# Halving additions, a copy on ScalarE and more first-load tiles in the block inverse of a recurrent attention with a mixture of experts

## The chip, the cores and the metric

The kernel runs on one core of a Trainium2 chip. The core has TensorE (PE, matrix multiplications, with PEld for its weight loads), VectorE (DVE), ScalarE (ACT), GpSimd (POOL) and SyncE (SP, which mostly issues DMA transfers). Each engine works through its own list of instructions in order and waits at an instruction whose operands are not ready. The metric is device time in microseconds (us) of one execution. Where the text speaks of the clock, it is the share of TensorE's full clock that the profile shows as granted.

## The reference

The inputs r, k, v, w, a and b have the shape (4 batches, 8 heads, 768 steps, 40 channels), float32. For each batch and head a state of 40 x 40 runs through the steps:

```python
for t in range(S):
    y[:, :, t] = einsum('bhd,bhde->bhe', rt, state)
    Sa = einsum('bhde,bhe->bhd', state, at)
    state = state * wt[:, :, None, :] - einsum('bhd,bhe->bhde', Sa, bt) + einsum('bhd,bhe->bhde', vt, kt)
```

The 3072 x 320 result goes through eight experts of two layers (320 to 1024, relu, 1024 to 320). Their outputs are summed with weights P, which come from x @ w_gate by eight rounds of normalising over rows and columns in turn.

## The kernel before, in words

**Chunks.** The 768 steps are cut into 12 chunks of 64. A pair of chunk c and batch b, numbered cb = 4c + b, is the unit of work; its eight heads are four pairs. There are two kinds of work for each unit.

**Preparation** (`prep`, line 106) does not depend on the state. It loads one block of 450 KB (line 109), makes the running products of the decays with two scans on VectorE (q, line 113, and gf, line 123), scales k, b and a with them (kb, line 137; ab, lines 143 and 144), multiplies them into a 64 x 64 triangle on TensorE (ll, line 149), transposes kb (kt, line 157) and writes masked copies into the tile set of that unit (sx, line 159; lines 145, 146 and 164 to 166). The lower triangle lt goes to DRAM (ld, lines 152 and 168). There are 20 tile sets. The first units have no tile of their own for the load: `IN_SEQ` lets units 0 to 3 load into sets 19 to 16, which no unit uses yet, units 4 and 5 into the two ordinary `inp` tiles, and units 6 and 7 into sets 19 and 18 again.

**Inverse.** For two chunks at a time (a group, `GROUPS`) the 32 x 32 diagonal blocks of all triangles, 128 in number, lie one to a partition: `load_lu` reads them from DRAM (lu, line 351), and VectorE inverts them (un). `inv_diag` (lines 171 to 177) does the 8 x 8 blocks column by column; `inv_off` then joins them with eight calls of `contract` (line 179) for a group, each with one product of 512, 1024 or 2048 elements for each partition (line 183, pr; four of 512, two of 1024 and two of 2048) and one reduction over the inner index (line 186). `finish` makes a turned copy tn, which lies in the same tile as pr (line 340), and writes un and tn to DRAM (ud and nd, lines 342 and 343). `tload` reads them back in the layout of the matrix multiplications (td and tt, lines 215 to 221) and `tmat` joins two 32 x 32 blocks into one 64 x 64 inverse on TensorE (gp, line 230; op, line 235).

**Recurrence** (`recur`, line 239). For each unit, in five steps with a yield between them: av (line 259), masked on VectorE into f (line 260); xc (line 267) with the set's sx; pu (line 278) with the inverse tt, masked into pm (line 280); c (line 285) with the set's bb, added into ws on VectorE (line 287); y and z on GpSimd (lines 291 and 302; z on VectorE from chunk 9); and the transpose zt (line 307), which carries the state on. Four batches go side by side.

**What sets the order.** The list `ev` (line 355) gives each piece of work a time on a scale where one chunk of recurrence is 5; the functions are called in that order, and a scheduler then places the instructions in each engine's list. `P0` and `PD` set the preparations of a group against the recurrence, `INV_DT` spaces the steps of an inverse, and `T_CLEAR` places the zeroing of fixed tiles. After the attention the experts follow; from their eighth block on, the order is the one in which the code is written.

Of the kernel before, what the change touches and what calls it, by code (L numbers as in the profile page):

```python
# [11 lines left out]
F32 = mybir.dt.float32  # L12
F32R = mybir.dt.float32r
AF = mybir.ActivationFunctionType
ALU = mybir.AluOpType
AX = mybir.AxisListType
# [4 lines left out]
NP = 4  # L21
R2 = 104
RP = 112
# [6 lines left out]
def attention(ctx, tc, d, xd, ps, pq, pt, gs, lg):  # L30
    nc = tc.nc
    pin = ctx.enter_context(tc.tile_pool(name="a_in", bufs=1))
# [19 lines left out]
    for n in range(NCH * NB - NSX, NCH * NB):  # L52
        i, pool = n % NSX, sets[n - NCH * NB + NSX]
        if i in IN_SETS or i in KB_SETS:
            raw = pool.tile([128, 1252], F32, name=f"st{i}")
# [19 lines left out]
    un, lu, tn = (t[:, 0:1024].rearrange("u (a b) -> u a b", b=32) for t in (unf, luf, prf))  # L75
# [5 lines left out]
    def clear():  # L81
        nc.gpsimd.memset(unf, 0.0)
        nc.gpsimd.memset(unf[:, 0:1024:33], 1.0)
        for t in vz_b + c1_b + lg_b:
            nc.vector.memset(t, 0.0)
        for t in tt_b:
            nc.gpsimd.memset(t, 0.0)
    fresh = set(range(NSX))

    def first_use(i):  # L90
        if i in fresh:
            fresh.discard(i)
            nc.gpsimd.memset(bb_b[i], 0.0)
            nc.scalar.copy(out=sx_b[i][64:R2].rearrange("r p h x -> r (p h) x")[:, :, 64:104],
                           in_=cst[64:R2, 360:400].unsqueeze(1).broadcast_to([40, 8, 40]))
# [3 lines left out]
    def rot(key, lst):  # L99
        i = state[key]  # L100
        state[key] = (i + 1) % len(lst)
        return lst[i]
# [3 lines left out]
    def prep(c, b, ld):  # L106
        cb = c * NB + b
        inp = raws[IN_MAP[cb]][0:RP, 0:1029] if IN_MAP.get(cb) else pin.tile([RP, 1029], F32, name="inp", bufs=2)
        nc.sync.dma_start(out=inp, in_=d["inp"][c, b])
        kb_in = inp[0:R2, 261:773].rearrange("r (p k t) -> r p k t", p=NP, k=2)  # L110
        a_in = inp[0:R2, 773:1029].rearrange("r (p t) -> r p t", p=NP)
        qf = pin.tile([RP, NP, 65], F32, name="q")
        nc.vector.tensor_tensor_scan(  # L113
            out=qf.rearrange("r p t -> r (p t)"), data0=inp[:, 0:260], data1=one65,
            initial=0.0, op0=ALU.mult, op1=ALU.add)
        q = qf[0:R2]
        g1 = rot("g1", g1_b)
        nc.vector.reciprocal(out=g1[:, :, 64], in_=qf[:, :, 64])
        sx = rot("sx", sx_b)
        i = next(j for j in range(NSX) if sx_b[j] is sx)  # L120
        bb, cc = bb_b[i], cc_b[i]
        gf = pin.tile([RP, NP, 65], F32, name="gf", bufs=2)
        nc.vector.tensor_tensor_scan(  # L123
            out=gf.rearrange("r p t -> r (p t)")[:, 259::-1], data0=inp[:, 260:0:-1],
            data1=g1.rearrange("r p t -> r (p t)")[:, 259::-1], initial=0.0, op0=ALU.mult, op1=ALU.add)
        gd[c, b] = dr1.tile([RP, 260], F32, name=f"gd{cb}")
        nc.sync.dma_start(out=gd[c, b], in_=gf.rearrange("r p t -> r (p t)"))
        g = gf[0:R2, :, 64:0:-1]
        if cb < NKB:
            raw = raws[KB_SETS[cb % len(KB_SETS)]]  # L130
            kb = raw[0:R2, 0:512].rearrange("r (p k t) -> r p k t", p=NP, k=2)
            lt = raw[0:64, 512:1024].rearrange("r (p k t) -> r p k t", p=NP, k=2)
        else:
            kb = pin.tile([R2, NP, 2, 64], F32, name="kb")
            lt = pin.tile([64, NP, 2, 64], F32, name="lt")
        eng = nc.vector if cb < NFAST else nc.gpsimd
        (nc.gpsimd if cb in KB_POOL else eng).tensor_tensor(
            out=kb, in0=kb_in,
            in1=q[:, :, 63::-1].unsqueeze(2).broadcast_to([R2, NP, 2, 64]), op=ALU.mult)
        ab = rot("ab", ab_b)  # L140
        first_use(i)
        nc.gpsimd.tensor_copy(out=cc, in_=q[:, :, 64])
        eng.tensor_tensor(out=ab[0:40, :, 0:64], in0=a_in[0:40], in1=g[0:40], op=ALU.mult)
        eng.tensor_tensor(out=ab[64:104, :, 64:128], in0=a_in[64:104], in1=g[64:104], op=ALU.mult)  # L144
        nc.scalar.copy(out=sx[64:104, :, 0, 0:64], in_=ab[0:40, :, 0:64])
        nc.scalar.copy(out=sx[64:104, :, 1, 0:64], in_=ab[64:104, :, 64:128])
        ll = pq.tile([128, NP, 2, 64], F32, name="ll", tag="pq")
        for p in range(NP):
            nc.tensor.matmul(ll[:, p], lhsT=kb[:, p], rhs=ab[:, p], start=True, stop=True)  # L149
        if cb < NKB:  # L150
            nc.scalar.activation(out=lt, in_=ll[64:128], func=AF.Copy, scale=-1.0)
            (nc.sync if cb < N_SP else nc.scalar).dma_start(out=ld[GRP[c][1], :, b], in_=lt)
            kt = pt.tile([128, NP, 2, 64], F32, name="kt", tag="pt")
        else:
            kt = pq.tile([128, NP, 2, 64], F32, name="kt", tag="pq")
        for p in range(NP):
            nc.tensor.transpose(kt[:, p].rearrange("s h x -> s (h x)")[:, 0:R2],
                                kb[:, p].rearrange("r k s -> r (k s)"), ident[0:R2, 0:R2])
        nc.vector.tensor_tensor(
            out=sx[0:64, :, :, 0:64], in0=ll[0:64],  # L160
            in1=mask_u.unsqueeze(1).unsqueeze(1).broadcast_to([64, NP, 2, 64]), op=ALU.mult)
        if cb >= NKB:
            nc.scalar.activation(out=lt, in_=ll[64:128], func=AF.Copy, scale=-1.0)
        nc.scalar.copy(out=sx[0:64, :, :, 64:104], in_=kt[0:64, :, :, 0:40])
        nc.scalar.activation(out=bb[0:64, :, 0:40], in_=kt[64:128, :, 0, 0:40], func=AF.Copy, scale=-1.0)
        nc.scalar.activation(out=bb[64:128, :, 64:104], in_=kt[64:128, :, 1, 0:40], func=AF.Copy, scale=-1.0)
        if cb >= NKB:
            (nc.sync if cb < N_SP else nc.scalar).dma_start(out=ld[GRP[c][1], :, b], in_=lt)
        return dict(cc=cc, sx=sx, bb=bb)
# [9 lines left out]
    def contract(us, dst, a, m):  # L179
        nu = us.stop - us.start  # L180
        n_c, n_r, n_k = a.shape[1], m.shape[2], a.shape[2]
        prv = prf[us, 0:n_c * n_r * n_k].rearrange("u (c k r) -> u c k r", r=n_r, k=n_k)
        nc.vector.tensor_tensor(  # L183
            out=prv, in0=a.unsqueeze(3).broadcast_to([nu, n_c, n_k, n_r]),
            in1=m.unsqueeze(1).broadcast_to([nu, n_c, n_k, n_r]), op=ALU.mult)
        nc.vector.tensor_reduce(out=dst, in_=prv.rearrange("u c k r -> u c r k"), op=ALU.add, axis=AX.X)  # L186

    def inv_off(us, o, n, h):
        gt = gtf[us, 0:n * n].rearrange("u (c r) -> u c r", r=n)
# [147 lines left out]
                   dr.tile([128, 32, 32], F32, name="ud"), dr.tile([128, 32, 32], F32, name="nd")]  # L337

    def finish(s, us):
        nc.vector.tensor_copy(out=tn[us], in_=un[us].rearrange("u c s -> u s c"))  # L340
        for o in range(0, us.stop, 64):
            nc.sync.dma_start(out=invs[s][1][o:o + 64], in_=un[o:o + 64])
            nc.sync.dma_start(out=invs[s][2][o:o + 64], in_=tn[o:o + 64])

    def load_lu(s, n):
        ld = invs[s][0]
        for cc in range(n):
            for blk in range(2):
                for h in range(2):
# [2 lines left out]
                        out=lu[u0:u0 + 16],  # L352
                        in_=ld[cc, r0:r0 + 32].rearrange("j b p h s -> (b p) j h s")[:, :, h, r0:r0 + 32])

    ev = [(T_CLEAR, clear, ())]
    gens = {}
    def step(c, b):
        if (c, b) not in gens:
# [8 lines left out]
    for c in range(NCH):  # L367
        for b in range(NB):
            for k in range(5):
                ev.append((5 * c + k + SKEW * b, step, (c, b)))  # L370
        t = 5 * c + 2 - T_LEAD
        ev.append((t - L_LEAD, tload, (c,)))
        for half in range(2):
            ev.append((t + 2 * SKEW * half, tmat, (c, half)))
    for s, cs in enumerate(GROUPS):
        us = slice(0, 64 * len(cs))
        t0 = 5 * cs[0] - 10
        n = len(cs) * NB
        for i in range(n):
            cb = (cs[0] + i // NB, i % NB)  # L380
            j = cb[0] * NB + cb[1] - NSX
            t = 5 * (j // 4) + 3 + SKEW * (j % 4) + 0.01
            t = max(t, t0 + P0 + PD * i) if s else -20 + 0.01 * i
            ev.append((t, do_prep, (s,) + cb + (i == 0,)))
        t += 0.02
        ev.append((t, load_lu, (s, len(cs))))
        for i, (fn, a) in enumerate(INV):
            ev.append((t + INV_DT * i, fn, (us,) + a))
        ev.append((t + INV_DT * 10 + 0.01, finish, (s, us)))
    for _, fn, args in sorted(ev, key=lambda x: x[0]):  # L390
# [5 lines left out]

GROUPS = [[0, 1], [2, 3], [4, 5], [6, 7], [8, 9], [10, 11]]
GRP = {c: (i, j) for i, g in enumerate(GROUPS) for j, c in enumerate(g)}
P0 = -8
PD = 0.75  # L400
INV_DT = 0.05
SKEW = 1.1
NSX = 20
GL = 1
# [2 lines left out]
NFB = 3  # L407
NRB = 2
KB_POOL = (1,2,3,4,5,6,7)
IN_SETS = (19, 18, 17, 16)  # L410
KB_SETS = (15, 14, 13, 12)
IN_SEQ = (19,18,17,16,0,0,19,18)
IN_MAP = dict(enumerate(IN_SEQ))
N_SP = 8
NKB = 6
NFAST = 6
T_CLEAR = -19.95
PC = 4
PQ = 2
PT = 2  # L420
T_LEAD = 2
L_LEAD = 0.5
NWS = 4
NK = (2 * E - 1) * (NF // 2)
# [386 lines left out]
```

## Time and profile before

| | us |
|---|---|
| median of 3 runs | 1846.83 (1845.23 to 1849.42) |
| the profiled execution, its own time | 1847.82 |
| its span, first to last instruction | 1846.0 |
| mean granted TensorE clock | 0.954 |
| TensorE busy in the span | 1734.9 |
| VectorE busy in the span | 1397.2 |

The page shows the span in 40 slices of 46 us; a digit is a tenth of the slice. The attention takes about the first eleven slices, where VectorE is as busy as TensorE or busier and the clock digit is under 9 in most of them; the experts take the rest, where TensorE is busy throughout. The span and the profiled execution's own time differ by 1.8 us, which lie around the span.

### The profile page before, as it was taken

Reading aid. Unit: us, or ns where it says so; the run is one execution under the profiler, and the core shown is the slowest. Engines: PE = TensorE matmul, PEld = TensorE weight load, DVE = VectorE, ACT = ScalarE, POOL = GpSimd, SP = SyncE. Lnnn points to the kernel's source line nnn. Section 1 sums busy time; section 2 is a strip of 40 time slices with the busy share of each in tenths; the row PEclk is TensorE's granted clock in tenths of the full one; section 3 lists DMA queues with packets and bytes.
Section 4 is the critical chain, followed back from the end, with each engine's and each line's share of the span. In section 5 each row is a group of like instructions: output and inputs, shape, how many; then the busy total and the mean of one; then the engine's idle time right before and its main releaser. Section 6 shows DMA issues by size and latency. Waiting matters only on the chain.

```text
span 1846.0 us, 31552 instructions
## 1 busy us (share of the span) xinstructions
PE 1734.9 (94%) x11843; PEld 1705.9 (92%) x11843; DVE 1397.2 (76%) x2306; ACT 855.9 (46%) x1848; POOL 873.1 (47%) x848
## 2 busy tenths in 40 slices
PE   5479898999989999999999999999999999999999
PEld 4378788899888999999999999999999999999999
DVE  7877969768698768677786868977686877778675
ACT  6347666666643534344343443445343443435342
POOL 6535556441572618355371826006291744628170
PEclk8569988889899999999999999999999999999999
DMA  8467787875720102011110202201020111102001
GB/s 211 116 152 177 184 183 181 182 173 133 203 82 31 56 1 75 20 56 38 38 56 19 75 20 67 65 14 57 19 75 19 57 38 38 57 19 75 5 34 43
DMA packets 194957, 145.10 MB, mean 79 GB/s; under 512 B 143861, under 2 KB 171637, under 8 KB 194805
## 3 DMA queue, kind: packets, MB, share of 16 engines
q1 hardware_dynamic: 191125, 137.35, 28.3%
q10 hardware_dynamic: 3680, 5.74, 1.1%
q8 instruction: 94, 1.54, 0.4%
q14 instruction: 58, 0.48, 0.1%
HBM read 117.00 MB, written 26.04 MB: 77 GB/s over the span
## 4 chain that ended last, share of the span: by engine, by line
PE 76%; DVE 10%; DMA 6%; issue 4%; ACT 2%; POOL 2%; SPq 1%; DVEq 0%; ACTq 0%; POOLq 0%
PE op L620 36%; PE p L555 33%; DMA inp<-in_inp_dram 2%; PE xc L267 2%; DVE pr L183 2%; DVE gt L186 1%; PE pu L278 1%; DVE q L113 1%; PE c L285 1%; PE av L259 1%; DVE un L186 1%; DMA ld<-lt 1%; DVE gf L123 1%; DMA rb<-in_r_dram 1%; DVE hl L579 1%
## 5 line engine op out<-in xcount | busy, mean ns | idle before, releaser
L555 PE MATMUL p<-xch,wh 128*128 128x384 f32 (+1 forms) x1792 | 605.7, 339 | 9.2 <-DVE sm L573 5.6
L576 ACT ACTIVATE hh<-sm 128x384 fp32r<-128x384 f32 x512 | 269.4, 526 | 726.4 <-DVE sm L573 726.2
L620 PE MATMUL op<-wh,hh 128*128 128x320 f32 x1536 | 476.8, 311 | 1.0 <-ACT hh L576 0.9
L620 PE MATMUL op<-wl,hh 128*128 128x320 f32 x1536 | 474.6, 309 | 0.0
L620 PE MATMUL op<-wh,hl 128*128 128x320 f32 x1536 | 467.1, 309 | 0.7 <-DVE hl L579 0.7
L501 POOL TENSOR_TENSOR wl<-ws,wh 128x640 fp32r<-128x640 f32 x60 | 103.6, 1727 | 608.5 <-ACT wh L499 608.3
L579 DVE SCALAR_TENSOR_TENSOR hl<-sm,hh 128x384 fp32r<-128x384 f32 x512 | 375.6, 767 | 2.4 <-ACT hh L576 2.0
L555 PEld LDWEIGHTS p<-xch,wh 128*128 128x128 f32 (+1 forms) x1792 | 337.4, 188 | 13.4 <-DVE sm L573 6.8
L555 PE MATMUL p<-xcl,wh 128*128 128x384 f32 x896 | 302.5, 338 | 0.0
L555 PE MATMUL p<-xch,wl 128*128 128x384 f32 x896 | 301.8, 337 | 0.0
L620 PEld LDWEIGHTS op<-wh,hh 128*128 128x128 f32 x1536 | 290.2, 189 | 1.6 <-ACT hh L576 1.5
L620 PEld LDWEIGHTS op<-wl,hh 128*128 128x128 f32 x1536 | 291.0, 189 | 0.0
L620 PEld LDWEIGHTS op<-wh,hl 128*128 128x128 f32 x1536 | 286.9, 188 | 1.1 <-DVE hl L579 0.9
L573 DVE TENSOR_TENSOR sm<-p,u 128x384 f32<-128x384 f32 x384 | 234.3, 621 | 8.8
L555 PEld LDWEIGHTS p<-xcl,wh 128*128 128x128 f32 x896 | 168.7, 188 | 0.0
L555 PEld LDWEIGHTS p<-xch,wl 128*128 128x128 f32 x896 | 168.6, 188 | 0.0
L573 DVE TENSOR_TENSOR sm<-p,p 128x384 f32<-128x384 f32 x128 | 71.2, 557 | 128.5 <-PE p L555 76.5
L573 DVE TENSOR_TENSOR p<-p,p 128x384 f32<-128x384 f32 x128 | 71.1, 555 | 98.7 <-PE p L555 98.0
L573 DVE TENSOR_TENSOR u<-p,p 128x384 f32<-128x384 f32 x128 | 70.8, 553 | 59.7 <-PE p L555 58.6
L509 POOL TENSOR_TENSOR wl<-ss,wh 128x512 fp32r<-128x512 f32 x60 | 89.9, 1498 | 32.7 <-ACT wh L506 28.4
L149 PE MATMUL ll<-ab,kb 104*128 104x128 f32 x336 | 64.0, 350 | 43.8 <-POOL ab L144 22.2
L291 POOL TENSOR_TENSOR y<-ws,gr 104x256 f32<-104x256 f32 x48 | 49.5, 1031 | 117.3 <-DVE ws L287 95.0
(156 smaller groups left out, 2774.4 us busy)
## 6 DMA issues: line engine op xcount, KB each, us to landing
ws<-in_wts_dram SPq DMA_DIRECT2D x60, 832.0 KB
inp<-in_inp_dram SPq DMA_DIRECT2D x42, 450.2 KB
rb<-in_r_dram SPq DMA_DIRECT2D x48, 224.0 KB
gd<-gf SPq DMA_DIRECT2D x48, 113.8 KB
gr<-gd SPq DMA_DIRECT2D x48, 113.8 KB
vz<-in_v_dram SPq DMA_DIRECT2D x48, 112.0 KB
ld<-lt ACTq DMA_DIRECT2D x40, 128.0 KB
f<-in_vt_dram SPq DMA_DIRECT2D x48, 80.0 KB
```

The lines of the kernel that those rows point to most:

```text
L149: nc.tensor.matmul(ll[:, p], lhsT=kb[:, p], rhs=ab[:, p], start=True, stop=True)
L183: nc.vector.tensor_tensor(out=prv, in0=a.unsqueeze(3).broadcast_to([nu, n_c, n_k, n_r]), in1=m.unsqueeze(1).broadcast_to([nu, n_c, n_k, n_ ...
L186: nc.vector.tensor_reduce(out=dst, in_=prv.rearrange("u c k r -> u c r k"), op=ALU.add, axis=AX.X)
L267: nc.tensor.matmul(xc[h][:, p], lhsT=pp["sx"][:, p, h], rhs=f[:, p, h], start=True, stop=True)
L291: nc.gpsimd.tensor_tensor(out=y[:, :, b % 2], in0=ws[:, :, 0:64], in1=gr[0:R2, :, 64:0:-1], op=ALU.mult)
L501: g.tensor_tensor(out=wl[:, 0:640], in0=raw[:, 256:896], in1=wh[:, 0:640], op=ALU.subtract)
L509: g.tensor_tensor(out=lv[:, 3:7], in0=so[:, :, 0], in1=hv[:, 3:7, 0], op=ALU.subtract)
L555: nc.tensor.matmul(o, lhsT=w_, rhs=x_, start=(j == 0), stop=(j == 3))
L573: eng.tensor_tensor(out=out, in0=x, in1=y, op=ALU.add)
L576: nc.scalar.activation(out=hh[:, f, h], in_=sm[f][:, h], func=AF.Relu)
L579: v.scalar_tensor_tensor(out=hl[:, f, h], in0=sm[f][:, h], scalar=0.0, in1=hh[:, f, h], op0=ALU.max, op1=ALU.subtract)
L620: nc.tensor.matmul(ops[i], lhsT=a[:, h, cs], rhs=w_[:, cw], start=(f == 0 and h == 0 and j == 0), stop=(last and h == 1 and j == 2))
```

## The change

It has these parts:

- In `contract` the reduction is replaced by halving additions: the inner index of n_k (8 or 16) is cut in half and the halves added, in place in pr, until one is left, which goes to the destination. A call with n_k = 8 issues three additions, one with 16 issues four.
- The turned copy tn in `finish` is made on ScalarE and not on VectorE.
- The first eight units each have a tile set to load into (sets 19 to 12), the sets that hold their kb and lt are 11 to 8, and all eight are prepared in the manner that was used for the first six (`NKB`, `NFAST`). The tile q has two buffers (`NQF`).
- The zeroing of un and of the VectorE tiles is placed at -20.01, that of tt in a function of its own at -19.915.
- The numbers that place the work: `P0` from -8 to -10, `INV_DT` from 0.05 to 0.2, and `T_FIRST` = 0 in place of 5 * 0 + 2 - 2 for chunk 0, which is the same value.

```diff
@@ attention
+    def clear_tt():
         for t in tt_b:
             nc.gpsimd.memset(t, 0.0)
@@ prep
-        qf = pin.tile([RP, NP, 65], F32, name="q")
+        qf = pin.tile([RP, NP, 65], F32, name="q", bufs=NQF)
@@ contract
-        nc.vector.tensor_reduce(out=dst, in_=prv.rearrange("u c k r -> u c r k"), op=ALU.add, axis=AX.X)
+        while n_k > 1:
+            n_k //= 2
+            nc.vector.tensor_tensor(out=dst if n_k == 1 else prv[:, :, 0:n_k],
+                                    in0=prv[:, :, 0] if n_k == 1 else prv[:, :, 0:n_k],
+                                    in1=prv[:, :, 1] if n_k == 1 else prv[:, :, n_k:2 * n_k], op=ALU.add)
@@ finish
-        nc.vector.tensor_copy(out=tn[us], in_=un[us].rearrange("u c s -> u s c"))
+        nc.scalar.copy(out=tn[us], in_=un[us].rearrange("u c s -> u s c"))
@@ the list of events
-    ev = [(T_CLEAR, clear, ())]
+    ev = [(T_CLEAR, clear, ()), (T_CLEAR2, clear_tt, ())]
-        t = 5 * c + 2 - T_LEAD
+        t = 5 * c + 2 - T_LEAD if c else T_FIRST
@@ the numbers
-P0 = -8
+P0 = -10
-INV_DT = 0.05
+INV_DT = 0.2
-IN_SETS = (19, 18, 17, 16)
-KB_SETS = (15, 14, 13, 12)
-IN_SEQ = (19,18,17,16,0,0,19,18)
+IN_SETS = (19, 18, 17, 16, 15, 14, 13, 12)
+KB_SETS = (11, 10, 9, 8)
+IN_SEQ = (19, 18, 17, 16, 15, 14, 13, 12)
-NKB = 6
-NFAST = 6
-T_CLEAR = -19.95
+NKB = 8
+NFAST = 8
+T_CLEAR = -20.01
+T_CLEAR2 = -19.915
+NQF = 2
+T_FIRST = 0
```

The scheduler places everything anew. Three places of its lists matter below; line numbers of the changed kernel are two to nine higher than those of the kernel before.

SP's list at the start of the program, before: st and inp are the loads of the units (a number behind st names the tile set), vz, rb and f the first tiles of the recurrence.

```order
L109 DMA st_173<-in_inp_dram 112x1029
L109 DMA inp<-in_inp_dram 112x1029 x2
L242 DMA vz_208<-in_v_dram 112x4x64
L245 DMA rb<-in_r_dram 112x512
L250 DMA f<-in_vt_dram 64x8x40
L242 DMA vz_209<-in_v_dram 112x4x64
L245 DMA rb<-in_r_dram 112x512
```

The same place in the changed kernel:

```order
L111 DMA st_164<-in_inp_dram 112x1029
L111 DMA st_163<-in_inp_dram 112x1029
L111 DMA st_162<-in_inp_dram 112x1029
L111 DMA st_161<-in_inp_dram 112x1029
L111 DMA inp<-in_inp_dram 112x1029 x2
L248 DMA vz_200<-in_v_dram 112x4x64
L251 DMA rb<-in_r_dram 112x512
L256 DMA f<-in_vt_dram 64x8x40
```

Ten unit loads, and not six, now stand ahead of the first vz and rb.

VectorE's list at the end of the first inverse, before: the reduction into un of 128x16x8 is the last step of the inverse, and the two rows of 128x4 begin the next inverse.

```order
L186 TENSOR_REDUCE un<-pr 128x16x8
L123 SCALAR_TENSOR_TENSOR gf<-inp,g_207 112x260
L113 SCALAR_TENSOR_TENSOR q<-inp,cst 112x260
L340 COPY pr<-un 128x1024
L118 RECIPROCAL g_207<-q 112x4
L123 SCALAR_TENSOR_TENSOR gf<-inp,g_207 112x260
L159 TENSOR_TENSOR st_172<-ll,cst 64x8x64
L159 TENSOR_TENSOR st_173<-ll,cst 64x8x64
L174 TENSOR_TENSOR pr<-un,lu 128x4
L177 TENSOR_REDUCE un<-pr 128x4
```

The same place in the changed kernel, from the last product of the first inverse on:

```order
L185 TENSOR_TENSOR pr<-gt,un 128x2048
L115 SCALAR_TENSOR_TENSOR q<-inp,cst 112x260
L161 TENSOR_TENSOR st_165<-ll,cst 64x8x64
L115 SCALAR_TENSOR_TENSOR q<-inp,cst 112x260
L190 TENSOR_TENSOR pr<-pr 128x16x64
L120 RECIPROCAL g_199<-q 112x4
L190 TENSOR_TENSOR pr<-pr 128x16x32
L125 SCALAR_TENSOR_TENSOR gf<-inp,g_199 112x260
L190 TENSOR_TENSOR pr<-pr 128x16x16
L120 RECIPROCAL g_199<-q 112x4
L190 TENSOR_TENSOR un<-pr 128x16x8
L125 SCALAR_TENSOR_TENSOR gf<-inp,g_199 112x260
```

The copy is gone from this list, four additions stand where one reduction stood, and rows of preparations stand between them. From the first row of the first inverse to its last, the list before holds five q, five gf and six sx rows, the changed one eight q, seven gf and eight sx rows. After one gf and one sx row the second inverse begins in the changed list, and the first row pm of the recurrence comes 34 rows behind that beginning; before, the first pm stood 19 rows behind it. The later inverses end, counted in units of the recurrence ahead of the first that needs them, 3, 5, 4, 4 and 4 units early in the changed list, and 4, 3, 3, 3 and 2 before.

TensorE's list between the first inverse and the first pu, before:

```order
L149 MATMUL ll<-ab_206,kb 128x128 x4
L157 MATMUL kt<-cst,kb 128x104 x4
L230 MATMUL gp<-td,lg 64x32 x8
L149 MATMUL ll<-ab_205,kb 128x128 x4
L157 MATMUL kt<-cst,kb 128x104 x4
L235 MATMUL op<-td,lg 64x32 x8
L230 MATMUL gp<-td,lg 64x32 x8
L278 MATMUL pu<-x_924,tt_201 128x104 x4
```

The same place in the changed kernel:

```order
L151 MATMUL ll<-ab_197,kb 128x128 x4
L159 MATMUL kt<-cst,kb 128x104 x4
L236 MATMUL gp<-td,lg 64x32 x8
L241 MATMUL op<-td,lg 64x32 x8
L236 MATMUL gp<-td,lg 64x32 x8
L284 MATMUL pu<-x_1019,tt_193 128x104 x4
```

The preparation that stood between gp and op is gone from there. Ahead of the first pu the list now holds the ll of 19 units, and before of 17.

## The prediction

> **What bounds the kernel now.** I read the page's slices first, then busy time by stage, then who is waited for in the stages that are not full. The clock's row of the page's slices (40 of 46 us each, tenths), below 9 only in the first eleven:
>
> ```profile
> PEclk8569988889899999999999999999999999999999
> ```
>
> Busy time in four of the five stages that I cut at the first inverse (55), the first pu (111), the first expert products (505) and the end of the transition; the columns are busy us of PE, PEld, DVE, ACT and POOL, granted clock, DMA share and GB/s:
>
> ```profile
> 0.00:55.00 55.00, 28.59 (x152) 25.38 (x152) 36.67 (x67) 33.27 (x81) 34.97 (x61) 0.78 0.84 203
> 55.00:111.00 56.00, 23.91 (x130) 21.70 (x131) 44.71 (x64) 19.66 (x50) 28.32 (x27) 0.50 0.50 121
> 111.00:505.00 394.00, 356.93 (x3236) 339.43 (x3235) 310.05 (x455) 260.74 (x647) 189.59 (x221) 0.89 0.75 176
> 650.00:1846.00 1196.00, 1192.07 (x7491) 1190.89 (x7489) 883.65 (x1500) 475.83 (x937) 539.76 (x464) 1.00 0.13 42
> ```
>
> Behind 650 TensorE is busy for 1192 of 1196 us at full clock, and the change touches nothing there: every gain or loss is made ahead of the experts. From 55 to 111 nothing but VectorE is full, and TensorE waits for the first inverse at half clock. From 111 to 505 TensorE is idle for 394 - 357 = 37 us, and the clock withholds another 0.11 x 394 = 43 us. So 80 us are the most that the recurrence could give back. Where it stalls, these rows of TensorE's timeline say (start, duration, the instruction, and in brackets the idle time and who ended it):
>
> ```profile
> 190.12 0.52 PE L307 MATMUL zt<-cst,z 104*40 104x104 f32 x4 [2.70 <-DVE un L177]
> 230.71 0.54 PE L307 MATMUL zt<-cst,z 104*40 104x104 f32 x4 [2.21 <-POOL z L302]
> 275.25 1.17 PE L259 MATMUL av<-rb,vz 104*104 104x128 f32 x8 [2.64 <-DVE ws L287]
> ```
>
> and these 10 us stretches, with the columns as above:
>
> ```profile
> 120.00:130.00 10.00, 7.59 (x41) 6.94 (x40) 9.90 (x15) 6.61 (x16) 4.33 (x5) 0.63 0.82 172
> 190.00:200.00 10.00, 8.15 (x58) 7.80 (x59) 9.86 (x19) 7.83 (x19) 5.89 (x9) 0.66 0.76 165
> 230.00:240.00 10.00, 9.29 (x60) 9.04 (x61) 9.97 (x13) 4.70 (x14) 5.86 (x7) 0.59 0.70 174
> 490.00:500.00 10.00, 8.16 (x44) 7.15 (x45) 9.49 (x15) 5.93 (x13) 7.04 (x7) 0.56 0.53 169
> ```
>
> VectorE is full there (9.5 to 10 of 10) in 22 of the 39 stretches from 110 to 500, of which the first and the last are shown, mostly while an inverse runs. A TensorE stall of two to three us is followed by a low clock: at 0.59 the ten us after 230 withhold 4.1 us more. An inverse thus costs the recurrence by standing in VectorE's list ahead of f, pm and ws.
>
> **The additions.** The groups of the reduction and of the product, by shape (count | busy, mean ns):
>
> ```profile
> L186 DVE TENSOR_REDUCE un<-pr 128x128 f32<-128x2048 f32 x6 | 23.1, 3849 | 0.0
> L186 DVE TENSOR_REDUCE gt<-pr 128x128 f32<-128x2048 f32 x6 | 21.6, 3605 | 0.0
> L186 DVE TENSOR_REDUCE gt<-pr 128x64 f32<-128x512 f32 x12 | 12.9, 1074 | 0.1
> L186 DVE TENSOR_REDUCE un<-pr 128x64 f32<-128x512 f32 x12 | 12.8, 1070 | 0.1
> L186 DVE TENSOR_REDUCE un<-pr 128x128 f32<-128x1024 f32 x6 | 12.0, 1994 | 0.0
> L186 DVE TENSOR_REDUCE gt<-pr 128x128 f32<-128x1024 f32 x6 | 11.3, 1876 | 0.0
> L183 DVE TENSOR_TENSOR pr<-gt,un 128x2048 f32<-128x2048 f32 x6 | 13.7, 2278 | 0.0
> L183 DVE TENSOR_TENSOR pr<-un,lu 128x512 f32<-128x512 f32 x12 | 9.5, 795 | 0.1
> L340 DVE COPY pr<-un 128x1024 f32<-128x1024 f32 x6 | 6.3, 1046 | 0.0
> ```
>
> and one of the short products in the timeline:
>
> ```profile
> 62.37 0.67 DVE L183 TENSOR_TENSOR pr<-un,lu 128x512 f32<-128x512 f32 x1
> ```
>
> The reductions take 93.7 us, 15.6 for each of six groups. No addition of SBUF data by halves is in the trace. The nearest rows are the products, also two-input operations: one of 512 took 0.67 us here, the mean of 2048 is 2.28, which is 0.13 us plus 1.05 ns an element. By that an addition of 1024, 512, 256, 128 or 64 takes 1.20, 0.67, 0.40, 0.26 or 0.20 us. The four calls of 512 need 0.86 us each, the two of 1024 1.33, the two of 2048 2.53: 11.2 us. With 26 instructions in place of 8, and 0.04 us from one to the next (so products and reductions follow each other in the timeline), it is 11.9. So 3.7 us a group are saved. The upper bound is 4.4 (no gap); the lower is a small loss, if each addition is stretched as the 512 products are, whose mean is 0.795 where this one took 0.67: 26 x 0.125 = 3.3 us eat nearly all. I take 3.7 less half of that stretch, 2.1, and 1.05 more for the copy that leaves VectorE: 3.2 us a group. On ScalarE the copy should cost about 1 us as on VectorE; it has room there (261 of 394 us busy).
>
> **The start.** The first inverse begins when lu lands, which hangs on the last of eight preparations. VectorE's wait there, and what held the first f up:
>
> ```profile
> 16.64 2.01 PE L259 MATMUL av<-rb,vz 104*104 104x128 f32 x8 [4.98 <-DMA rb<-in_r_dram]
> 18.69 0.69 DVE L260 TENSOR_TENSOR f<-av,cst 104x512 f32<-104x512 f32 x1 [3.00 <-PE av L259]
> 42.53 0.70 DVE L113 TENSOR_TENSOR_SCAN q<-inp,cst 112x260 f32<-112x260 f32 x1 [2.40 <-POOL kb L137]
> 55.04 0.16 DVE L174 TENSOR_TENSOR pr<-un,lu 128x4 f32<-128x4 f32 x1 [2.18 <-DMA lu<-ld]
> ```
>
> The eight own load tiles and the second q remove waits like the one at 42.5. But the changed list has ten loads of 450 KB ahead of rb and not six. Those six and what goes with them are 3.4 MB, landed by 16.6; four more at the same 0.24 MB a us end 7 us later, so the first av ends at about 25.5 and f waits on VectorE until then, with the preparations 3 to 7 queued behind it. Those (five q and gf, ten ab, four sx, one f) are 14 to 16 us by their durations, so the eighth ab comes at about 41, ll and lt 3 us later, and ld to DRAM and lu back in 8 us as before (47.3 to 55.0). The inverse starts at about 53: **-2 us**. Bounds: -10 (the loads arrive before VectorE gets to f), +2.
>
> **The first inverse** took 55.0 to 95.4, 40.3 us with VectorE hardly idle. It saves 2.1 by the additions, but takes in three more q, two more gf and two more sx, about 0.6 us each in the stream, 4.6 with their reciprocals: **+2 us**, from -2 to +6. That preparation work is not lost: it need not be done later.
>
> **From un to the first pu**, on VectorE, SP and TensorE:
>
> ```profile
> 91.59 3.80 DVE L186 TENSOR_REDUCE un<-pr 128x128 f32<-128x2048 f32 x1
> 97.54 1.09 SPq L343 DMA_DIRECT2D nd<-pr  x2
> 100.47 0.86 SPq L215 DMA_DIRECT2D td<-nd  x2
> 103.68 1.91 PE L230 MATMUL gp<-td,lg 64*64 64x32 f32 x16 [1.77 <-DMA td<-ud]
> 105.52 2.07 PE L149 MATMUL ll<-ab,kb 104*128 104x128 f32 x8
> 108.22 1.59 PE L235 MATMUL op<-td,lg 64*64 64x32 f32 x13
> 111.37 2.03 PE L278 MATMUL pu<-x,tt 128*128 128x104 f32 x8
> ```
>
> un was done at 95.4 (91.59 + 3.80), nd went out 2.1 us later, because gf and q stood ahead of the copy on VectorE. On ScalarE the copy follows un at once: 1 us less. The ll and kt between gp and op are gone: op was 2.7 us behind gp's end and needs a copy of 0.7, so 1.8 less. **-3 us**, bounds -4 and 0 (ScalarE still in a preparation). The second inverse, next in VectorE's list, must now wait until nd has read the shared tile; nothing of the recurrence waits behind it, since its first pm is 14 us off.
>
> **Work moved ahead.** Two more units have their ll and kt done before the first pu; at full clock they are 1.16 and 0.52 us (the row of 147.08 in the timeline):
>
> ```profile
> 147.08 1.16 PE L149 MATMUL ll<-ab,kb 104*128 104x128 f32 x8 [0.48 <-POOL ab L144]
> 148.08 0.52 PE L157 MATMUL kt<-cst,kb 104*128 104x104 f32 x4
> ```
>
> That is **-3 us** of TensorE work, moved to where TensorE idles; bounds -5 and 0.
>
> **The recurrence.** Five inverses lose 3.2 us each on VectorE, 16 us, and their pieces are at most 2.3 us and not 3.8. Most of the first 15 us of the second inverse now lie ahead of the first pm: 12 us more. Of these 28, 22/39 fall where VectorE is full, 16; since not every full stretch holds a stall, I credit 9. **-9 us**; bounds -35 (nearly half of the 80) and +16 (the first rival).
>
> Sum: -2 + 2 - 3 - 3 - 9 = -15. From the profiled execution's 1847.8 that is 1832.8; the median of the runs is 1.0 lower, so **1832**.
>
> **Rivals.** 1) *Slower: the additions lock GpSimd out.* What speaks for it:
>
> ```profile
> 73.20 2.27 DVE L183 TENSOR_TENSOR pr<-un,lu 128x2048 f32<-128x2048 f32 x1
> 73.34 2.17 POOL L142 COPY st<-q 104x4 f32<-104x4 f32 x1 [2.33 <-DVE q L113]
> 81.96 1.87 DVE L186 TENSOR_REDUCE gt<-pr 128x128 f32<-128x1024 f32 x1
> 83.27 0.19 POOL L142 COPY st<-q 104x4 f32<-104x4 f32 x1
> ```
>
> The same small copy took 2.17 us under a product and 0.19 under a reduction. The additions' 12 us a group replace reductions, under which GpSimd was free; z on GpSimd may stand still under them, and zt, av and f behind it. The Trainium skill has this as a rule (SBUF — State Buffer, Who interferes with whom): an operation with two SBUF inputs excludes a GpSimd operation that reads SBUF for its whole length, a reduction never does; the rows agree. One stall as at 230.7 costs 2.2 + 4.1 = 6.3 us. One more for each of the five later inverses is 31: 1832 + 31 = 1863. From three on (19) the gain is gone. Against it: the additions are short, and zt waited for z only twice in 394 us (the list of TensorE's waits from 111 to 505, with total, times and longest; 230.7 is one):
>
> ```profile
> PE zt L307 <- POOL z L302: 3.5, 2, 2.2
> ```
>
> 2) *The recurrence keeps its stalls*, because others (transfers, the copies on ScalarE) take their place, with the DMA share at 0.75: only the first four terms, -6: 1841. 3) *The start gives it all back*: the first loads crowd out rb and the handover to the experts (clock 0.56 at 490) shifts by as much as was gained: 1846. 4) *The stalls behind VectorE go for the most part*, as the inverses now end 3 to 5 units early and not 2 to 4: 25 us in place of 9: 1816.
>
> **How the numbers follow.** Chances: my forecast 0.40, rival 1 0.14, rival 2 0.21, rival 3 0.10, rival 4 0.15. The range runs from 1812 (rival 4 and a little) to 1849 (rival 3 and the mildest part of rival 1). My forecast's own range is 1822 to 1840. A measurement of this kernel tells about 0.2%, 3.7 us, from no change. Faster: 0.38 + 0.19 + 0.15 + 0.02 = 0.74; same: 0.10; slower: 0.16.
>
> **What would show it.** In the changed profile: additions of line 190 in sum near 13.5 us a group; the first L176 at 51 to 55; gp to op without ll and the first pu at 107 to 109; fewer stretches with VectorE at 10 and a clock above 0.89 from the first pu to the experts. GpSimd's z at over 0.6 us in the mean, and zt waiting for it, would speak for rival 1. The prediction is wrong if the stage of the recurrence is no shorter, or if the first f comes before 20 us and the start gains 8 or more.

## The result, and the profile after

The changed kernel takes 1861.2 us (median of 6, 1854.3 to 1865.5) beside 1848.3 us for the kernel before on the same chip (median of 6, 1845.2 to 1852.5): a ratio of 1.0067, with a 95% interval of 1.0046 to 1.0087. So it is slower by some 12 us, where 15 us less had been forecast. The profiled execution spans 1856.6 us, 10.6 more than the one of before.

The clock's row of the page's slices, after, and busy time in the stretches that the prediction showed of the kernel before (busy us of PE, PEld, DVE, ACT and POOL, granted clock, DMA share, GB/s):

```profile
PEclk8559897999899999999999999999999999999999
```

```profile
0.00:55.00 55.00, 30.57 (x152) 26.75 (x152) 39.47 (x72) 33.25 (x81) 34.06 (x58) 0.82 0.83 204
55.00:111.00 56.00, 24.14 (x106) 21.70 (x107) 49.06 (x86) 23.48 (x55) 33.56 (x35) 0.50 0.50 129
111.00:505.00 394.00, 353.30 (x3162) 335.02 (x3160) 285.44 (x525) 259.40 (x627) 202.09 (x213) 0.87 0.75 170
650.00:1846.00 1196.00, 1196.00 (x7517) 1195.39 (x7516) 881.51 (x1503) 478.10 (x941) 547.54 (x473) 1.00 0.13 42
```

The experts are untouched, at full clock. From 111 to 505 VectorE has 285 us of work and not 310, as was meant, though 7 of these 25 us have only moved ahead of 111 (88.5 us there beside 81.4). TensorE is no busier for it (353 of 394 us, 357 before), and its clock is 0.87 and not 0.89.

The first steps, in the timeline after:

```profile
22.76 2.01 PE L265 MATMUL av<-rb,vz 104*104 104x128 f32 x8 [1.82 <-DMA rb<-in_r_dram]
55.32 0.17 DVE L176 TENSOR_TENSOR pr<-un,lu 128x4 f32<-128x4 f32 x1 [0.81 <-DMA lu<-ld]
102.94 0.65 DVE L190 TENSOR_TENSOR un<-pr 128x128 f32<-128x128 f32 x1
103.62 1.97 ACT L346 COPY pr<-un 128x1024 f32<-128x1024 f32 x1 [4.25 <-DVE un L190]
105.61 1.09 SPq L349 DMA_DIRECT2D nd<-pr  x2
112.88 1.89 PE L236 MATMUL gp<-td,lg 64*64 64x32 f32 x16 [1.24 <-DMA td<-nd]
115.59 1.59 PE L241 MATMUL op<-td,lg 64*64 64x32 f32 x13 [0.82 <-ACT lg L238]
118.74 2.03 PE L284 MATMUL pu<-x,tt 128*128 128x104 f32 x8
```

The first inverse starts where it did (55.3 beside 55.0) but ends at 103.6, 8.2 us later, and the first pu comes at 118.7, 7.4 later. That is not lost outright: TensorE used part of the time for preparations. When the first pu starts, 307 matmuls have ended, and before it was 283. At the mean price of each kind (busy time multiplied by the clock) in the kernel before behind 120, the 24 more are 2.7 us, an estimate. By the same prices the changed kernel is 2.8 us behind at 120 (312 matmuls ended, 346 before), 10.4 at 200 and 11.0 at 700: most of the loss arises between 120 and 200. Busy time multiplied by the clock does not show the first part: up to 120 it is 39.8 us after and 39.5 before, but the same 152 matmuls of the first 55 us count 24.6 us in it after and 20.8 before. From 110 to 700, in one row for each kernel, before and then after:

```profile
110.00:700.00 590.00, 541.32 (x4400) 518.97 (x4398) 466.17 (x741) 347.12 (x820) 281.41 (x306) 0.92 0.55 133
```

```profile
110.00:700.00 590.00, 538.78 (x4348) 515.30 (x4348) 436.83 (x808) 347.30 (x809) 282.92 (x289) 0.90 0.56 131
```

TensorE's idle time there is 590 - 541.3 = 48.7 us before and 51.2 after. The clock is 0.92 and 0.90: summed in pieces of 10 us (busy time by one less the clock) it withholds 39.9 us before and 48.3 after. In the experiments I call these two sums **idle** and **withheld**. By them 2.5 us are stalls and 8.4 the low clock, but they take in the wait for the first pu, and the pieces of 10 us are coarse. At the clock's own steps (last section) and from 120 to 700, idle is 48.6 us before and 49.2 after, withheld 40.9 and 46.3. So the stalls hardly grew in sum; the clock took more behind them. The remaining 2.2 us of the lag behind 120 are matmuls that took longer.

TensorE's longest lists of waits in the recurrence (from 111 to 505: us in total, times, longest), before and after:

```profile
PE ll L149 <- POOL ab L144: 4.0, 5, 1.9
PE xc L267 <- DVE f L260: 3.8, 4, 1.9
PE av L259 <- DVE ws L287: 3.8, 3, 2.6
```

```profile
PE op L241 <- ACT lg L238: 7.6, 5, 4.0
PE ll L151 <- POOL ab L146: 6.9, 3, 4.2
PE ll L151 <- POOL kb L139: 6.2, 5, 1.8
PE zt L313 <- POOL z L308: 3.3, 2, 2.5
```

VectorE's rows are gone from the head of the list. ScalarE (op waits for its copy lg) and GpSimd (ll waits for kb and ab) have taken their place. One of these waits, seen on ScalarE (timeline, after), and on TensorE:

```profile
183.43 0.50 ACT L279 COPY x<-xc 64x416 f32<-64x416 f32 x1 [0.53 <-ACT lt L165]
183.94 0.50 ACT L280 COPY c<-xc 40x416 f32<-40x416 f32 x1
184.45 0.32 ACT L261 COPY f<-z 40x160 f32<-40x160 f32 x1
...
186.91 0.30 ACT L168 ACTIVATE bb<-kt 64x160 f32<-64x160 f32 x1
187.22 0.36 ACT L237 COPY lg<-gp 32x256 f32<-32x256 f32 x1
```

```profile
182.90 1.08 PE L236 MATMUL gp<-td,lg 64*64 64x32 f32 x16 [0.74 <-DMA td<-nd]
188.00 1.91 PE L241 MATMUL op<-td,lg 64*64 64x32 f32 x16 [4.01 <-ACT lg L238]
```

gp ended at 184.0, but its copy lg stood behind copies x, c, f, x, c, sx and bb in ScalarE's list, and op behind it waited 4.0 us. The delay begins further back, on VectorE:

```profile
180.91 0.17 DVE L176 TENSOR_TENSOR pr<-un,lu 128x4 f32<-128x4 f32 x1 [3.41 <-DMA lu<-ld]
181.60 0.67 DVE L161 TENSOR_TENSOR sx<-ll,cst 64x512 f32<-64x512 f32 x1
182.31 0.59 ACT L165 ACTIVATE lt<-ll 64x512 f32<-64x512 f32 x1 [2.03 <-DVE sx L161]
```

The first row of the next inverse stood in VectorE's list and waited for lu; sx came behind it, ScalarE's lt waited for sx, and the copies stood behind lt. That wait is not new: from 111 to 505 VectorE waited 7.9 us for lu before and 3.4 after. Here it counts by what stood behind it. Here is TensorE in the same place, cut at the steps of 3.41 us in which the clock changes (length, busy us, clock):

```profile
178.95:182.36 3.41, 3.03 (x29) 1.00 0.77 124
182.36:185.78 3.42, 1.08 (x16) 1.00 0.80 159
185.78:189.19 3.41, 1.19 (x11) 0.50 0.77 159
189.19:192.60 3.41, 3.41 (x20) 0.50 0.98 222
192.60:196.02 3.42, 3.42 (x20) 0.50 1.04 205
196.02:199.43 3.41, 2.75 (x27) 1.00 0.73 155
```

One step with 1.08 us of work, and the next three are at half clock. The 4.0 us of stall cost another 4.0 of clock ((1.19 + 3.41 + 3.42) / 2).

### The profile page after: what moved, and what is told of

Read it like the earlier page. It is cut to its first block, busy times and chain, and to the rows that moved or that the text cites. A ratio compares the mean times of both kernels' runs of the same rounds, so it can differ in the third digit from the quotient of the medians.

```text
span 1856.6 us, 31660 instructions
## 1 busy us (share of the span) xinstructions
PE 1745.1 (94%) x11843; PEld 1714.5 (92%) x11843; DVE 1377.9 (74%) x2412; ACT 866.8 (47%) x1854; POOL 889.0 (48%) x844
## 4 chain that ended last, share of the span: by engine, by line
PE 75%; DVE 3%; DMA 2%; ACT 1%; issue 1%; POOL 1%; SPq 0%; DVEq 0%; POOLq 0%; ACTq 0%
PE op L629 36%; PE p L564 33%; PE xc L273 2%; PE pu L284 1%; PE av L265 1%; PE c L291 1%; DMA inp<-in_inp_dram 1%; DVE hl L588 1%; PE op L241 1%; PE gp L236 0%; PE lp L323 0%; DVE sm L582 0%; DMA ld<-lt 0%; PE zt L313 0%; DMA xs<-xd 0%
## 5 line engine op out<-in xcount | busy, mean ns | idle before, releaser
L588 DVE SCALAR_TENSOR_TENSOR hl<-sm,hh 128x384 fp32r<-128x384 f32 x512 | 371.0, 758 | 2.4 <-ACT hh L585 2.0
L151 PE MATMUL ll<-ab,kb 104*128 104x128 f32 x320 | 63.3, 355 | 48.9 <-POOL kb L139 19.5
L151 PEld LDWEIGHTS ll<-ab,kb 104*128 104x128 f32 x320 | 54.0, 253 | 53.8 <-POOL kb L139 31.8
```

What stands on the lines that cost most here:

```text
L588: v.scalar_tensor_tensor(out=hl[:, f, h], in0=sm[f][:, h], scalar=0.0, in1=hh[:, f, h], op0=ALU.max, op1=ALU.subtract)
```

## The experiments

Each is compared with runs of the kernel before on the same chip, whose median lay between 1847.8 and 1849.1. The theories: **A**, the additions lock GpSimd out (the first rival); **B**, the start with its eight preparations costs; **C**, the later places of preparations and inverse steps cost; **D**, each part has a price of its own, the copy on ScalarE above all; **E**, the order of the lists decides: each edit makes the scheduler write new lists, other stalls come up, and the clock takes more than the stalls themselves.

### One part of the change undone, or done alone

Reductions back, in the changed kernel:

```diff
-        while n_k > 1: ... (halving additions)
+        nc.vector.tensor_reduce(out=dst, in_=prv.rearrange("u c k r -> u c r k"), op=ALU.add, axis=AX.X)
```

> The changed kernel with the reduction put back in place of the halving additions, all else as changed. If the additions lock GpSimd out (theory A), GpSimd's kb and z fall back to about 1.29 and 0.5 us in the mean, TensorE's waits for kb and ab from 13 to about 6 us, and the time to 1845 to 1850, although VectorE has some 20 us more of work. If the start is the cause (theory B: eight preparations ahead of and within the first inverse), the first pu stays at 118 or later, since the longer reductions lengthen the first inverse too, and the time is 1861 to 1868. If the later times of the inverse are the cause (theory C), about 1861.

1859.1 us, 1.0059 (1.0036 to 1.0082). The loss stays without a single addition: A is not its cause, although z falls back to 0.55 and 0.52 us and TensorE's waits for kb and ab, from 111 to 505, to 4.0 us from 13.1 (kb itself stays at 1.44 us). The first inverse is 6 us shorter than with the additions (54.3 to 96.3), with six q, five gf and six sx in it and not eight, seven and eight, and the first pu comes at 115.0, so B's 118 was wrong too.

Additions alone, in the kernel before:

```diff
-        nc.vector.tensor_reduce(out=dst, in_=prv.rearrange("u c k r -> u c r k"), op=ALU.add, axis=AX.X)
+        while n_k > 1: ... (halving additions)
```

> The kernel before with the halving additions alone. Theory A: slower than before by 5 to 13 us (1853 to 1861), with kb, ab and z longer on GpSimd. Theories B and C: not slower than before; the first inverse ends 2 to 4 us earlier and the time is 1840 to 1848.

1849.6 us, 1.0011 (0.9994 to 1.0029): no difference that can be told. What A describes does happen. GpSimd's z, from 0 to 510, took 0.48 and 0.55 us in the mean before (lists of line 302), and with the additions:

```profile
L306 POOL TENSOR_TENSOR z<-ws,cc 104x160 f32<-104x160 f32 x20 | 16.1, 806 | 0.0
L306 POOL TENSOR_TENSOR z<-ws,st 104x160 f32<-104x160 f32 x16 | 12.2, 761 | 0.0
```

TensorE's waits for kb and ab grow from 5.7 to 9.6 us (111 to 505), those for z do not (1.6 us in 3 waits, 3.5 in 2 before), and the time does not follow. The first inverse takes 47.8 us here as well, with seven q, eight gf and eight sx in it, and not the 2 to 4 less that B and C expected.

The two constants as before, in the changed kernel:

```diff
-P0 = -10
-INV_DT = 0.2
+P0 = -8
+INV_DT = 0.05
```

> The changed kernel with the two constants of the order (earliest time of a preparation, distance of an inverse's steps) as before. Theory C: back to about 1848. Theories A and B: 1858 to 1864, the first pu still at 118 and GpSimd's kb still at 1.45 us in the mean.

1861.6 us, 1.0081 (1.0057 to 1.0105): C falls.

The loads, early preparations and zeroing as before, in the changed kernel:

```diff
-IN_SETS = (19, 18, 17, 16, 15, 14, 13, 12)
-KB_SETS = (11, 10, 9, 8)
-IN_SEQ = (19, 18, 17, 16, 15, 14, 13, 12)
+IN_SETS = (19, 18, 17, 16)
+KB_SETS = (15, 14, 13, 12)
+IN_SEQ = (19,18,17,16,0,0,19,18)
... (NKB, NFAST 8 to 6; T_CLEAR, T_CLEAR2 to -19.95; NQF 2 to 1)
```

> The changed kernel with the places of the loads, the counts of early preparations, the second q and the zeroing as before; additions, copy and constants as changed. Theory B: the first pu at 107 to 111 in place of 118.7 and a time of 1846 to 1852, more than half of the loss. Theories A and C: the first pu earlier too, but the loss behind it stays: 1855 to 1862.

1863.9 us, 1.0087 (1.0064 to 1.0110), with the first pu at 118.0 although the first av is back at 16.2: B falls. All slow kernels so far had the copy on ScalarE, which led to the next four.

The copy back on VectorE, in the changed kernel:

```diff
-        nc.scalar.copy(out=tn[us], in_=un[us].rearrange("u c s -> u s c"))
+        nc.vector.tensor_copy(out=tn[us], in_=un[us].rearrange("u c s -> u s c"))
```

> The changed kernel with the turned copy back on VectorE, all else as changed. In the first four runs every kernel with the copy on ScalarE was slow (1859 to 1864) and the one without it was not. Theory D, the copy on ScalarE is the cause: 1846 to 1851. Theory A+B, additions and start together, with the copy innocent: 1857 to 1862.

1854.5 us, 1.0038 (1.0022 to 1.0054): between the two, half of the loss gone.

The copy on ScalarE alone, in the kernel before (the same edit the other way round):

```diff
-        nc.vector.tensor_copy(out=tn[us], in_=un[us].rearrange("u c s -> u s c"))
+        nc.scalar.copy(out=tn[us], in_=un[us].rearrange("u c s -> u s c"))
```

> The kernel before with the turned copy on ScalarE and nothing else. Theory D: 1856 to 1862, the first pu at 114 or later, and TensorE waiting for ScalarE's lg. Theory A+B: 1845 to 1850.

1862.9 us, 1.0078 (1.0061 to 1.0095). The time is as D says, but the place is not: the first pu comes at 113.1, and up to 285 the kernel stays near the one before (1.9 us behind, by the prices of the section before). Then pu waits 3.9 us at 293.7 for the copies x and c, which stand in ScalarE's list behind a copy that waits for GpSimd's ab; the turned copy is not near. What follows is in the last section.

Copy on VectorE and reductions back, in the changed kernel, so that loads, early preparations, zeroing and constants are left:

```diff
-        nc.scalar.copy(out=tn[us], ...)
+        nc.vector.tensor_copy(out=tn[us], ...)
-        while n_k > 1: ...
+        nc.vector.tensor_reduce(out=dst, ...)
```

> The changed kernel with both the copy on VectorE and the reduction back, so that only the loads, the early preparations, the zeroing and the two constants differ from before. Theory D: 1844 to 1850. If the additions do cost something that the rest gives back, this is faster than the kernel with the copy alone put back, by 2 us or more.

1863.8 us, 1.0085 (1.0062 to 1.0109), 9 us slower than with the additions (1854.5). D expected 1844 to 1850, since neither of the two parts it blames, the copy on ScalarE and the additions, is in this kernel.

A second copy on ScalarE into a place that nobody reads, in the kernel before:

```diff
         nc.vector.tensor_copy(out=tn[us], in_=un[us].rearrange("u c s -> u s c"))
+        nc.scalar.copy(out=prf[us, 1024:2048].rearrange("u (a b) -> u a b", b=32), in_=un[us].rearrange("u c s -> u s c"))
```

> The kernel before with its copy on VectorE as it was, and in addition the same copy on ScalarE into a place that nobody reads. If it is ScalarE's time (six copies of 2 us in front of the recurrence's own copies) that costs, 1855 to 1862, as with the copy on ScalarE; if it is what waits for the copy's data (the transfers to nd and td behind it), no slower than before, 1845 to 1851.

1860.6 us, 1.0076 (1.0055 to 1.0096). By its own terms this speaks for ScalarE's time. But this kernel too has new lists, so theory E was formed and tested.

### The order alone

Loads of tt and td due earlier, in the kernel before; no instruction has another shape or engine:

```diff
-L_LEAD = 0.5
+L_LEAD = 1
```

> The kernel before with one number of the order changed (the loads of tt and td are due 1 step and not half a step ahead of their use): no instruction's cost or engine differs, only the order in the engines' lists. Theory E (the order before is a favourable one; a new order brings some other TensorE stalls of three us and more, and the clock takes the rest): 1853 to 1862, with 45 us or more of clock withheld from 110 to 700 (40 in the kernel before) and idle time about as before (46 to 56). Theory D (each part's own cost): 1845 to 1851, since nothing is added.

1854.7 us, 1.0036 (1.0020 to 1.0052). Preparations at 0.8 of a step:

```diff
-PD = 0.75
+PD = 0.8
```

> The kernel before with the distance of preparations at 0.8 and not 0.75 of a step: the order alone changes, by about as many rows as with the copy on ScalarE. Theory E: 1853 to 1862, clock withheld 45 us or more. Theory D: 1845 to 1851.

1857.3 us, 1.0043 (1.0022 to 1.0065). So an order alone costs 6 to 9 us. Idle is 47 us in both, no more than before (48.7); withheld is 58.0 and 53.6 (39.9 before). The profiled execution of the first took 1861.8 us, 7 more than its median, so its sums are high for that kernel; that of the second took 1856.4. The first of them, from 110 to 700:

```profile
110.00:700.00 590.00, 542.94 (x4319) 521.64 (x4319) 456.74 (x726) 339.45 (x807) 270.13 (x296) 0.89 0.54 132
```

P0 at -10, in the kernel before (INV_DT moves no row of its lists):

```diff
-P0 = -8
+P0 = -10
```

> The kernel before with the earliest time of a preparation at -10 and not -8, which is the change's one effective constant by itself (the other moves no row here): the order alone changes. Theory E: 1853 to 1862. Theory D: 1843 to 1851, as preparations come no later than before.

1849.1 us, 1.0003 (0.9990 to 1.0015): here E was wrong, an order can be new and as good. Loads, early preparations and zeroing alone, in the kernel before:

```diff
-IN_SETS = (19, 18, 17, 16)
+IN_SETS = (19, 18, 17, 16, 15, 14, 13, 12)
... (KB_SETS, IN_SEQ, NKB, NFAST, NQF, T_CLEAR, T_CLEAR2 as in the change)
```

> The kernel before with the places of the eight loads, the counts of early preparations, the second q and the zeroing of the change; reduction, copy on VectorE and constants as before. Theory D with the copy as the cause: 1844 to 1851. Theory E: 1853 to 1864. Theory B (crowding at the start): first av at 22 or later, first pu at 114 or later, 1852 to 1860.

1849.9 us, 1.0022 (1.0002 to 1.0042), although the first pu is at 118.1, as late as in the changed kernel. With P0 at -10, which by itself costs nothing, the same edit took 1863.8 above. The prices of parts do not add.

### The same instructions under other orders

A small extra copy on ScalarE in place of the dummy copy:

```diff
+        nc.scalar.copy(out=prf[us, 1024:1056], in_=unf[us, 0:32])
```

> The kernel before with one more copy on ScalarE behind each inverse, of 32 elements in place of the 1024 of the dummy copy, at the same place and waiting for the same data. If ScalarE's 2 us cost (theory D): 1846 to 1851, some 10 us under the dummy copy. If it is the wait in ScalarE's list or the order (theory E): 1853 to 1862.

1852.8 us, 1.0024 (1.0006 to 1.0041): between both expectations. The copy on ScalarE in the kernel before, with P0 = -10:

```diff
-        nc.vector.tensor_copy(out=tn[us], ...)
+        nc.scalar.copy(out=tn[us], ...)
-P0 = -8
+P0 = -10
```

> The kernel before with the turned copy on ScalarE, under another order: the earliest time of a preparation at -10. By itself that number moved nothing in the time (1849). Theory D: again 1859 to 1866. Theory E: anywhere from 1847 to 1866; below 1855 it would say that the copy has no price of its own of over 7 us.

1854.9 us, 1.0029 (1.0010 to 1.0049), 8 us less than the same copy under the other order. The dummy copy with P0 = -10:

```diff
+        nc.scalar.copy(out=prf[us, 1024:2048]..., in_=un[us]...)
-P0 = -8
+P0 = -10
```

> The kernel before with the dummy copy of 2 us on ScalarE, under the order with the earliest preparation at -10, with which the kernel before took 1849 and the copy on ScalarE 1855. If ScalarE's time costs by itself: 1857 to 1863 again. If the 12 us of the dummy copy came with its order: 1848 to 1856.

1847.7 us, 1.0006 (0.9991 to 1.0021). The 12 us of the dummy copy are gone with its order; ScalarE still does six copies of 2 us more than the kernel before. The two orders of the same instructions, from 110 to 700, first the slow one:

```profile
110.00:700.00 590.00, 544.31 (x4334) 521.41 (x4333) 458.85 (x730) 350.80 (x815) 272.87 (x297) 0.89 0.55 132
```

```profile
110.00:700.00 590.00, 538.59 (x4428) 516.09 (x4428) 466.64 (x745) 357.06 (x828) 286.73 (x308) 0.93 0.56 133
```

The faster one has more idle time (51.4 beside 45.7 us) and less withheld (34.0 beside 55.1). D falls in the form that 2 us of ScalarE's time have a fixed price.

The changed kernel under two more orders, first:

```diff
-PD = 0.75
+PD = 0.7
```

> The changed kernel under another order: preparations at a distance of 0.7 and not 0.75 of a step; every instruction stays the same. Theory D: 1858 to 1864, as the changed kernel. Theory E: a shift of 4 us or more to either side, with clock withheld from 110 to 700 moving with it.

and then:

```diff
-SKEW = 1.1
+SKEW = 1.2
```

> The changed kernel under a third order: units 1.2 and not 1.1 steps apart; every instruction stays the same. Theory D: 1858 to 1864. Theory E: a shift of 4 us or more to either side.

1863.2 us, 1.0077 (1.0054 to 1.0100), and 1865.6 us, 1.0087 (1.0067 to 1.0106). E expected shifts of 4 us or more; they are 2 and 4, both upward, and the two intervals overlap that of the changed kernel. Additions and copy on ScalarE together, in the kernel before:

```diff
-        nc.vector.tensor_reduce(out=dst, ...)
+        while n_k > 1: ...
-        nc.vector.tensor_copy(out=tn[us], ...)
+        nc.scalar.copy(out=tn[us], ...)
```

> The kernel before with the halving additions and the copy on ScalarE, and nothing else of the change. If the two together are the cause of the change's loss: 1858 to 1864. If the prices of parts do not add and each order has its own: below 1856 or above 1866 is as likely.

1855.8 us, 1.0052 (1.0034 to 1.0071): about 7 of the 12 us, and less than the 1858 expected if the two were the whole cause.

## Why the prediction was wrong

**What the runs show, and what stays open.** The time of these kernels follows the clock. Over the profiled executions of all twenty kernels, the span goes with withheld at a correlation of 0.83 (0.85 us of span for one of withheld), and with idle at 0.34. Both are parts of the span, so this says where the time lies and not what brings it there. It does not hang on the executions that were profiled: over the medians of all runs of the nineteen other kernels, the time goes with the part of the span that the mean clock takes away at 0.82. Idle from 110 on is 42 to 56 us everywhere; withheld runs from 34 to 58. Which stalls arise, and so what is withheld, changes with the order: by 1, 6 and 9 us in three orders with no instruction changed, by 8 and 13 us between two orders of the same edited instructions. None of the nineteen other kernels is faster than the kernel before; by the intervals three are as fast and sixteen slower, whatever was edited. That is shown. Not settled is whether the change's instructions have a price beside it. All six kernels that hold both the additions and the copy on ScalarE lost 0.5 to 0.9%, under six orders; the other thirteen that I made lost from nothing to 0.9%. So a few us may belong to the two together; no order was found that clears them. Nor is a price of the copy on ScalarE alone excluded: the nine kernels with it lost 0.3 to 0.9%, and of the ten without it five lost less than 0.25%.

By the prediction's own steps, in the profiled executions:

- *Start, -2*: the inverse begins at 55.3 (+0.3). The first av came at 22.8, where 23.5 had been reckoned from its end of 25.5: the crowding was sized rightly, the gain behind it did not come.
- *First inverse, +2*: +7.9 (40.4 to 48.3 us). This step failed. The list took in eight q, seven gf and eight sx in place of five, five and six, as reckoned. By the timeline they and the reciprocals hold VectorE for 19.5 us in place of 11.8: the three, two and two cost 7.7 and not 4.6, since a q takes 0.86 us and a gf 0.83 in the mean and not 0.69. The additions, put at 2.1 us less, saved 0.4 there (with the diagonal's reductions they take 16.7 us, all reductions before 17.1), and the products took 11.8 us in place of 10.4.
- *un to the first pu, -3*: -0.8 (16.0 to 15.2). The copy takes 1.97 us on ScalarE and not 1, so that nd goes out 2.0 us behind un as before.
- *Work moved ahead, -3*: -2.7, by the estimate above. The first four steps thus came to +4.7 in place of -6.
- *Recurrence, -9*: +5.9, what is left of the 10.6, and this is the step on which the forecast fell most. The stage from the first pu to the last zt took 397.4 us (118.7 to 516.1) and 390.1 before (111.4 to 501.5), the sign that the prediction had named for being wrong. Its first half was right in kind: VectorE's work shrank, and TensorE's waits for f (3.8 to 1.9 us) and ws (3.8 to 2.1) went down. Six groups of additions of line 190 take 83.8 us, 14.0 a group (forecast 13.5), where the reductions took 15.6; with products at 10.9 in place of 10.3 and the copy gone, VectorE saves 2.0 us a group and not 3.2. The wrong part was to credit freed VectorE time as stalls that vanish. TensorE's idle time stayed as it was (48.6 and 49.2 us from 120 to 700): the waits passed to ScalarE and GpSimd, whose lists were written anew, and the clock withheld 46.3 us behind them and not 40.9. VectorE was also less of a limit than the page was read to say: its digit reaches TensorE's in five of the first eleven slices, not in most.

The groups behind these sizes, after (count | busy, mean ns):

```profile
L190 DVE TENSOR_TENSOR pr<-pr 128x256 f32<-128x256 f32 x48 | 24.6, 513 | 0.5
L190 DVE TENSOR_TENSOR pr<-pr 128x512 f32<-128x512 f32 x24 | 17.4, 724 | 0.0
L190 DVE TENSOR_TENSOR pr<-pr 128x1024 f32<-128x1024 f32 x12 | 16.0, 1335 | 0.0
L190 DVE TENSOR_TENSOR pr<-pr 128x128 f32<-128x128 f32 x24 | 10.1, 422 | 0.2
L346 ACT COPY pr<-un 128x1024 f32<-128x1024 f32 x6 | 11.9, 1989 | 4.4 <-DVE un L190 4.2
```

An addition of 1024 was put at 1.20 us and takes 1.34; one of 256 at 0.40, and takes 0.51.

**The rivals.** The first gave 1863, close to the measured time, but that is luck: the sign named for it came (z at 0.69 and 0.95 us in the changed kernel, 0.76 to 0.81 under the additions alone) and TensorE's waits for kb and ab grow, but the additions alone made no difference that can be told, and the loss stays with the reductions back. The second, that other stalls take the place of VectorE's, is what the waits show. Its price of -6 kept the four terms of the start, which came to +4.7, and left out that the new stalls bring more clock loss (5.4 us from 120 to 700). The third had the shift at the start right in kind, but not as what decides: the loads alone had it and lost 0.2%. The fourth did not happen. The range had no case in which the order itself costs, though the prediction showed, at 230.7, that a stall of 2.2 us brought 4.1 us of clock.

## What to carry to other kernels

Where a scheduler writes the lists anew at every edit and TensorE waits close behind four engines, change only the order first (one number of the plan) and see how far the time moves; a forecast from durations that is smaller than this spread says little. Judge a saving by TensorE's idle time and by the clock withheld together, and look in the new lists at what stands ahead of each copy that TensorE waits for. An edit that looks bad under one order should be tried under a second before its instructions are blamed.

## What was not expected of the hardware

**The clock.** In all twenty traces TensorE's clock changes in steps of 3.41 us and is either full or half. I cut the traces from 100 to 640 us at these steps. Of full-clock steps in which TensorE was busy for less than half of the time, 126 of 127 were followed by half clock; at 0.5 to 0.6 it was 52 of 78, at 0.6 to 0.7 35 of 98, at 0.7 to 0.8 22 of 142, at 0.8 to 0.9 9 of 223, and at 0.9 or more 14 of 1776. So 1.5 us of idle time within one step can be enough. The way back is longer than the stall accounts for. The copy on ScalarE alone, at its stall of 3.9 us, shows it:

```profile
286.34:289.75 3.41, 3.41 (x40) 1.00 1.07 264
289.75:293.16 3.41, 0.11 (x2) 1.00 0.51 121
293.16:296.58 3.42, 2.88 (x13) 0.50 0.64 175
296.58:299.99 3.41, 3.41 (x25) 0.50 0.43 114
...
313.64:317.06 3.42, 3.42 (x20) 0.50 0.58 150
```

TensorE was fully busy from 296.6 on and still had half clock until 317. After a step at half clock in which TensorE was busy for less than 0.85 of the time the next was full in none of 142 cases. After a fully busy one (0.95 or more) it was full in about half (267 of 513), and about as often after the first such step in a row as after the second or fourth. Of the 256 drops that lie wholly in the cut 85 lasted one step, 96 two and 75 three to ten. What decides the return no run here shows; it may be why executions of one kernel differ (those of the kernel before lay between 1843.2 and 1855.7 us in 34 runs of one chip), but that is not shown. The Trainium skill (TensorE: Matmul & The Clock Gate, "HAM oscillation — how this bites in real kernels" and Part 1) warns of idle gaps above about 3.4 us and puts the return after at least one busy window. The length of the step agrees; in these traces gaps of half that length can suffice, and one busy window brought the clock back only in about half of the cases.

**A copy of 1024 elements** that reads in turned order takes 1.99 us on ScalarE and 1.05 on VectorE.
